# Two state decays moved behind the masks, one key decay moved ahead, and one quarter of a later group put in another order

## The chip, the cores and the metric

The kernel runs on one core of a Trainium2 chip. The metric is device time in microseconds (us) of one execution. The engines named below are TensorE (PE, matmuls; its weight loads are listed as PEld), VectorE (DVE), ScalarE (ACT), GpSimd (POOL) and SyncE (SP, here only a queue that issues DMAs). Each engine takes its instructions strictly in the order in which the code issues them, and waits at an instruction until what it reads is written and what it overwrites has been read.

## The reference

A linear attention with decay runs over 4 batches x 8 heads x 768 positions x 64 dimensions, and its output goes through a dense layer pair with a Mish between. Cut to what matters:

```
for b in range(nb):                                   # blocks of the sequence
    intra = (qb @ kb.T) * Dmask                       # masked scores inside the block
    intra = intra @ vb
    inter = (qb * lam_pow) @ kv_state                 # what the state of the blocks before gives
    out[block] = intra + inter
    kb_dec = kb * rev_pow                             # decayed keys
    kv_state = lam_block * kv_state + kb_dec.T @ vb   # decayed state
x = out as (3072 tokens, 512)
h = x @ w_in                                          # 512 -> 2048
out = (h * tanh(log1p(exp(h)))) @ w_out               # Mish, 2048 -> 512
```

## The kernel before

The sequence is cut into six **groups** `n` = 0 to 5 of 128 positions. In each group there are four **chunks** `b`, one for each batch, so that a group holds 512 tokens. The order of all work is written out by hand in one long body: what stands earlier in the code is issued earlier on each engine. There is no loop over equal stages that a scheduler reorders.

For a chunk `(n, b)` the attention goes in these steps. `decay_k` (L248) multiplies the keys by their decays into `kd`. `scores` (L255) puts eight small products into the PSUM banks `be` and `bo`, and two DVE multiplications with the mask `dm` (L260) write `sb`; these two are called the masks below. `outputs` (L276, L281) multiplies queries by the state and `sb` by the values into one bank, and a DVE multiplication (L284) writes `xn`; `xn` is turned on PE (L293, the function put aside in `later`) or by a DMA transpose (L287) into `xt`. `state` (L302) multiplies `kd` by the values; DVE adds the old state into `raw` (L310), and a last multiplication by `lbm` gives the new state `w0` to `w3` (L312), here called a state decay. In the second group (`n` = 1) the state decays of chunks 0 and 1 are put aside in the list `decays1` and run on DVE; those of chunks 2 and 3 run on POOL at once. `raw` has two buffers.

The first dense layer works on a group's 2048 features in units. In the second group each `two_units` puts eight matmuls of 256 columns into one of the banks `bA`, `bB`, `bC` and one Mish on ACT (L358) empties it. From the fourth group on the layer is done in four **quarters** (`set_of`, `set_step`) with seven products each in place of eight (Strassen's scheme): the steps `m1` to `m7` are four matmuls each (L412). `m5`, `m6`, `m7` and `m4` read differences of the input, `xsum0` to `xsum3` (L390, `x_sums`), of which the second and the fourth are built on earlier ones. Step `m5` copies its product to `p5` on ACT (L434), `m6` adds `p5` into bank C on DVE (L437), `m7` writes `c22` (L441).

The second dense layer of group `n` (`dense2`) runs beside the first layer of group `n` + 1 and the attention of group `n` + 2. It is a list of fourteen **halves**, eight matmuls each (L523), taken one after the other by `h(...)`: two each for the products 1, 2, 6, 5, 7, 3, 4. Products 6, 5, 7 and 3 read sums of the Mish outputs, `gsum0` to `gsum3` (L486, `sums`). The loop over `n` has one turn for each group; in the turn with `n` = 2 the fourth group's first layer starts, and it is the first turn whose quarters are of the kind "s" (seven products), after a turn whose last quarter was of the kind "p" (plain units). In that turn POOL prepares the keys of the fifth group (L248).

Of the kernel before, what the change touches and what calls it, by code (L numbers as in the profile page):

```python
# [7 lines left out]
F32 = mybir.dt.float32  # L8
# [5 lines left out]
def bc(ap, axis, n):  # L14
    shape = list(ap.shape)
    shape.insert(axis, n)
    return ap.unsqueeze(axis).broadcast_to(shape)
# [3 lines left out]
def kernel(  # L21
# [10 lines left out]
    nc = tc.nc  # L32
# [3 lines left out]
    JP = H // 2  # L36
# [14 lines left out]
    work = ctx.enter_context(tc.tile_pool(name="work", bufs=1))  # L51
    ps = ctx.enter_context(tc.tile_pool(name="ps", bufs=1, space=bass.MemoryType.PSUM))

    def bank(tag, shape, dtype=F32):
        return ps.tile([128] + shape, dtype, name=f"b{tag}", tag=f"b{tag}")
# [160 lines left out]
    def flat(t, j):  # L216
        return t[:, 2 * j : 2 * j + 2, :].rearrange("p h c -> p (h c)")
# [3 lines left out]
    def turn_pe(n, b, banks, which="kq", by_vector=False):  # L221

        srcs = (kn[n, b], qn[n, b])
        for src, name, to, tag in zip(srcs, ("kT", "qT"), (kT, qT), banks):
            if name[0] not in which:
                continue
            pt = bank(tag, [JP, C], F16)
            for j in range(JP):
                nc.tensor.matmul(pt[:, j, :], flat(src, j), ident, is_transpose=True,
                                 start=(j == 0), stop=(j == JP - 1))  # L230
            if b % 2 == 0:
                turned[name, n] = work.tile([128, 2 * JP, C], F16, name=name, tag=name, bufs=2)
            to[n, b] = turned[name, n][:, b % 2 * JP : b % 2 * JP + JP, :]
            if by_vector:
                nc.vector.tensor_copy(to[n, b], pt)
            else:
                nc.scalar.activation(to[n, b], pt, AF.Copy)
# [8 lines left out]
    def decay_k(n, b, eng):  # L246
        kd[n, b] = work.tile([128, H, D], F16, name="kd", tag="kd", bufs=4)
        eng.tensor_tensor(out=kd[n, b], in0=kn[n, b], in1=bc(lk, 2, D), op=ALU.mult)  # L248
# [23 lines left out]
    def outputs(n, b, turn=None, tag="z"):  # L272

        po = bank(tag, [H, D])
        for j in range(JP):
            nc.tensor.matmul(  # L276
                po[:, 2 * j : 2 * j + 2, :].rearrange("p h e -> p (h e)"), qT[n, b][:, j, :],
                wst[n, b][:, j, :], start=(j == 0), stop=False, skip_group_check=True)
        for j in range(JP):
            for t in range(2):  # L280
                nc.tensor.matmul(po[:, 2 * j + t, :], sb[n, b, t][:, j, :], vn[n, b][:, 2 * j + t, 0:D],  # L281
                                 start=False, stop=True, skip_group_check=True)
        xn = work.tile([128, H, D], F16, name="xn", tag="xn", bufs=2)
        nc.vector.tensor_tensor(out=xn, in0=po, in1=bc(lq, 2, D), op=ALU.mult)  # L284
        dst = x_tile(n)[:, :, b * C : (b + 1) * C]
        if turn is None:
            nc.sync.dma_start_transpose(out=dst, in_=xn.rearrange("p h c -> p (h c)"))  # L287
            return None

        def later():  # L290
            pt = bank(turn, [JP, C], F16)
            for j in range(JP):
                nc.tensor.matmul(pt[:, j, :], flat(xn, j), ident, is_transpose=True,  # L293
                                 start=(j == 0), stop=(j == JP - 1))
            nc.scalar.activation(dst, pt, AF.Copy)

        return later

    def state(n, b, tag, eng, later=False):
        pv = bank(tag, [JP, 128])  # L300
        for j in range(JP):
            nc.tensor.matmul(  # L302
                pv[:, j, :].rearrange("p (a e) -> p a e", a=2), flat(kd[n, b], j),
                vn[n, b][:, 2 * j : 2 * j + 2, 0:D], start=True, stop=True)
        w_new = const.tile([128, JP, 128], F16, name=f"w{b}") if n == 0 else wst[n, b]
        if n == 0:
            nc.vector.tensor_tensor(out=w_new, in0=pv, in1=lbm, op=ALU.mult)
        else:
            raw = work.tile([128, JP, 128], F32, name="raw", tag="raw", bufs=2)
            nc.vector.tensor_tensor(out=raw, in0=pv, in1=wst[n, b], op=ALU.add)  # L310
            wst[n + 1, b] = w_new
            decay = lambda: eng.tensor_tensor(out=w_new, in0=raw, in1=lbm, op=ALU.mult)  # L312
            return decay if later else decay()
        wst[n + 1, b] = w_new
# [3 lines left out]
    def h_tile(n):  # L318
        if n not in hsg:
            hsg[n] = work.tile([128, NKI, GT], F16, name="hsg", tag="hsg", bufs=2)  # L320
        return hsg[n]
# [22 lines left out]
    def next_bank():  # L344
        ring[0] += 1
        return "ABC"[ring[0] % 3]

    def two_units(n, ni, r):

        t = bank(next_bank(), [2, HC])  # L350
        cs = slice(r * HC, r * HC + HC)
        for u in range(2):
            for kc in range(NKC):
                m = (ni + u) % 4 * 128
                nc.tensor.matmul(  # L355
                    t[:, u, :], win[ni // 4][:, kc, m : m + 128], xt[n][:, kc, cs],
                    start=(u == 0 and kc == 0), stop=(kc == NKC - 1), skip_group_check=True)
        nc.scalar.activation(h_tile(n)[:, ni : ni + 2, cs], t, AF.Mish)  # L358
# [112 lines left out]
    def token_sum(n, i, part):  # L471

        if (n, i) not in gsum:
            gsum[n, i] = work.tile([128, HK, HC], F16, name=f"gsum{i}", tag=f"gsum{i}", bufs=1)
        w = HK // 2
        ks = slice(part * w, part * w + w)
        kh = slice(HK + part * w, HK + part * w + w)
        h = hsg[n]
        lo, hi = slice(0, HC), slice(HC, 2 * HC)
        a, b, op = (  # L480
            lambda: (h[:, ks, hi], h[:, kh, hi], ALU.add),
            lambda: (gsum[n, 0][:, ks, :], h[:, ks, lo], ALU.subtract),
            lambda: (h[:, ks, lo], h[:, ks, hi], ALU.subtract),
            lambda: (h[:, kh, lo], gsum[n, 1][:, ks, :], ALU.subtract),
        )[i]()
        nc.vector.tensor_tensor(out=gsum[n, i][:, ks, :], in0=a, in1=b, op=op)  # L486
# [187 lines left out]
    def sums(n, part, *which):  # L674
        for i in which:
            token_sum(n, i, part)

    ring[0] = 1
    later = {}

    def turn1(b, banks, eng=True):
        turn_pe(1, b, banks, "k")
        turn_pe(1, b, banks, "q", eng)

    def out1(b, turn, po, pv):
        later[b] = outputs(1, b, turn, po)
        return state(1, b, pv, nc.vector if b < 2 else nc.gpsimd, b < 2)

    first_units(8)
    for t in "kqv":  # L690
# [15 lines left out]
    decays1 = [out1(0, "G", "z", "H")]  # L706
# [7 lines left out]

    turn1(2, "ze")
    turn1(3, "oB")
    two_units(1, 0, 0)
    scores(1, 2)
    for decay in decays1:
        decay()  # L720
    decay_k(1, 2, nc.vector)
    two_units(1, 2, 0)
    two_units(1, 4, 0)
    scores(1, 3)
# [2 lines left out]
    two_units(1, 6, 0)  # L727
    later[2]()
    out1(3, "G", "e", "o")
    two_units(1, 8, 0)  # L730
    later[3]()
    two_units(1, 10, 0)
# [70 lines left out]
    def h(m=1):  # L803
        for _ in range(m):
            halves.pop(0)()
# [5 lines left out]
    KINDS = {1: "pppp", 2: "ssss", 3: "ssss", 4: "ssss"}  # L811
    WSUMS = {(1, 0): (1,), (1, 1): (3,)}

    for n in range(1, NG - 1):
# [32 lines left out]
        def fetch(*what):  # L847
            if m + 1 < NG:
                for t, bp in what:
                    load_pair(t, m + 1, bp)  # L850
# [6 lines left out]
        kinds = KINDS[n]  # L857
# [8 lines left out]
        def mm(i, *steps):  # L866
            for x in steps:
                set_step(sets[i], x)
# [5 lines left out]
        def opening(i):  # L874

            if kinds[i] == "s":
                mm(i, "m1")
                s_(i)
                mm(i, "seed")
                if i != 1:  # L880
                    settle()
            elif i == 0:
                s_(i)

        def closing(i):
            mm(i, "m7", "m3")
            owed.append(i)
# [35 lines left out]
            continue  # L923


        if "s" in kinds:
            x_sums(n + 1, 0, 1, 2, 3)
        opening(0)
        if m < NG:
            turn_dma(m, 1)  # L930
        if kinds[0] == "s":
            h(1)
            mm(0, "m2", "m5", "m6")
            sums(n, 1, 0, 1)
            h(1)
            o_(0)
            fetch(("k", 0), ("q", 0))
            closing(0)
        else:
            u(0)  # L940
            sums(n, 1, 0, 1)
            if n == 1:
                weight_sum(3, 0)
                weight_sum(3, 1)
            h(1)
            u(1)
            h(1)
            u(2)
            o_(0)
            fetch(("k", 0), ("q", 0))  # L950
            u(3)


        opening(1)
        h(1)
        if kinds[1] == "s":
            settle()
            mm(1, "m2")
# [121 lines left out]
```

## Time and profile before

| what | value |
|---|---|
| time, median of 3 runs | 205.52 us (205.46 to 206.92) |
| time of the profiled execution | 206.36 us |
| span from its first to its last instruction | 204.6 us |
| busy: PE, DVE, ACT, POOL | 193.8, 147.5, 98.5, 81.7 us |
| mean granted clock of TensorE | 0.999 |

A page of the profile lists busy times, shares by slices of the span, the chain of work that ended last, and groups of instructions. A row of the timeline gives the start and the length in us, the engine, the line, the operation with `out<-in`, and in brackets how long the engine had been idle before and on what. Buffer numbers are left out of names, so `w<-raw,lbm` stands for each of the four state decays, `p` for `p5` and `c` for `c22`. Lengths of matmuls include a tail in which the next one already runs; the distance of starts is what an instruction takes.

### The profile page before, as it was taken

The numbers are of one execution on the slowest core, as the hardware profiler recorded it, in microseconds if no ns is written. First come the engines' busy times: TensorE is split into PE (matmuls) and PEld (weight loads), VectorE is DVE, ScalarE is ACT, GpSimd is POOL, SyncE is SP. The second block draws the span as 40 slices with busy tenths as digits, with TensorE's granted clock in tenths as the row PEclk, the third lists the DMA queues.
The fourth block names the chain that finished last, engine by engine and source line by source line (L and its number), as shares of the span: only waits on it lengthen the run. The fifth ranks groups of instructions, "written<-read, shape, count | busy, mean of one in ns | idle before, by whom it ended". The sixth has DMA issues, their size and how long they took to land.

```text
span 204.6 us, 4668 instructions
## 1 busy us (share of the span) xinstructions
PE 193.8 (95%) x1931; PEld 149.1 (73%) x1931; DVE 147.5 (72%) x247; ACT 98.5 (48%) x176; POOL 81.7 (40%) x78
## 2 busy tenths in 40 slices
PE   7869998979999999999999999999999999999990
PEld 3657455768865556667668888988988988888890
DVE  6696557698896977589868698799588657179041
ACT  4775663728631125343245662465474484826300
POOL 7998452472272591648684368230000000000020
PEclk9999999999999999999999999999999999999999
DMA  8999999999999999699999999994113211003123
GB/s 129 137 142 204 175 177 156 162 207 194 142 141 131 223 167 176 159 108 115 161 212 194 137 77 130 172 211 112 29 26 80 77 54 53 0 3 113 47 100 104
DMA packets 109336, 26.26 MB, mean 128 GB/s; under 512 B 99458, under 2 KB 108802, under 8 KB 109314
## 3 DMA queue, kind: packets, MB, share of 16 engines
q0 software_dynamic: 77568, 13.37, 88.5%
q1 hardware_dynamic: 30704, 12.33, 29.0%
q10 hardware_dynamic: 1042, 0.26, 0.6%
q8 instruction: 15, 0.25, 0.5%
q14 instruction: 7, 0.06, 0.1%
HBM read 27.26 MB, written 6.29 MB: 164 GB/s over the span
## 4 chain that ended last, share of the span: by engine, by line
PE 76%; DMA 9%; POOL 7%; DVE 3%; ACT 2%; issue 1%; POOLq 0%; DVEq 0%; ACTq 0%
PE bG L523 15%; PE bH L523 13%; DMA vn<-in_v_dram 8%; PE bB L412 6%; PE bC L412 5%; PE bA L412 4%; PE bA L329 3%; PE bB L329 3%; PE be L255 2%; PE bC L355 2%; POOL win L96 2%; PE bC L329 2%; PE bz L281 2%; PE bA L574 2%; PE bA L355 2%; PE bB L355 2%
## 5 line engine op out<-in xcount | busy, mean ns | idle before, releaser
L312 POOL TENSOR_TENSOR w<-raw,lbm 128x512 f16<-128x512 f32 x14 | 20.4, 1458 | 43.0 <-DVE raw L310 42.8
L523 PEld LDWEIGHTS <-gsum 128*128 128x128 f16 x336 | 31.2, 98 | 4.3
L523 PEld LDWEIGHTS <-hsg 128*128 128x128 f16 x240 | 23.0, 98 | 4.4
L605 POOL TENSOR_TENSOR c<-p,u 128x512 f32<-128x512 f32 x1 | 1.3, 1272 | 58.7 <-DVE p L604 58.7
L260 DVE TENSOR_TENSOR sb<-be,dm 128x512 f16<-128x512 f32 x22 | 15.1, 686 | 8.8 <-PE bo L255 8.1
L523 PE MATMUL bH<-tsum,gsum 128*128 128x256 f16 x160 | 20.4, 273 | 0.0
L329 PEld LDWEIGHTS <-win 128*128 128x128 f16 x136 | 12.6, 98 | 10.3 <-DMA win<-in_moe_w_in_dram 0.5
L412 PEld LDWEIGHTS <-wsum 128*128 128x128 f16 x192 | 18.5, 98 | 2.1
L523 PE MATMUL bG<-wout,hsg 128*128 128x256 f16 x160 | 19.9, 273 | 0.0
L412 PEld LDWEIGHTS <-win 128*128 128x128 f16 x144 | 13.8, 98 | 2.2 <-issue 0.5
L486 DVE TENSOR_TENSOR gsum<-hsg 128x1024 f16<-128x1024 f16 x20 | 15.1, 759 | 0.0
L284 DVE TENSOR_TENSOR xn<-bz,lq 128x512 f16<-128x512 f32 x18 | 12.3, 686 | 3.7 <-PE bz L281 3.7
L260 DVE TENSOR_TENSOR sb<-bo,dm 128x512 f16<-128x512 f32 x22 | 15.0, 680 | 0.0
L355 PEld LDWEIGHTS <-win 128*128 128x128 f16 x128 | 12.0, 98 | 1.6
L87 POOL DMA_DIRECT2D kn<-in_k_dram x10 | 11.8, 1182 | 2.8 <-PE bB L329 1.5
L87 POOL DMA_DIRECT2D qn<-in_q_dram x10 | 11.7, 1170 | 1.7 <-PE bA L329 0.9
L87 POOL DMA_DIRECT2D vn<-in_v_dram x10 | 11.6, 1164 | 1.4 <-DMA win<-in_moe_w_in_dram 1.4
L412 PE MATMUL bA<-xt,win 128*128 128x256 f16 x80 | 12.0, 272 | 0.1
L416 ACT ACTIVATE hsg<-bC 128x512 f16<-128x512 f32 x10 | 5.9, 593 | 11.7 <-PE bC L412 11.7
L329 PE MATMUL bA<-xt,win 128*128 128x512 f16 x44 | 11.3, 380 | 0.0
L574 PEld LDWEIGHTS <-hsg 128*128 128x128 f16 x64 | 6.1, 98 | 6.8
L335 ACT ACTIVATE hsg<-bA 128x512 f16<-128x512 f32 x11 | 6.6, 597 | 9.2 <-PE bA L329 9.2
(189 smaller groups left out, 442.3 us busy)
## 6 DMA issues: line engine op xcount, KB each, us to landing
out_dram<-osum SPq DMA_DIRECT2D x23, 256.0 KB, 2.8
kn<-in_k_dram POOLq DMA_DIRECT2D x10, 256.0 KB, 9.0
qn<-in_q_dram POOLq DMA_DIRECT2D x10, 256.0 KB, 7.1
vn<-in_v_dram POOLq DMA_DIRECT2D x10, 256.0 KB, 8.6
wout<-in_moe_w_out_dram POOLq DMA_DIRECT2D x4, 512.0 KB, 15.4
win<-in_moe_w_in_dram POOLq DMA_DIRECT2D x3, 512.0 KB, 10.8
vz<-in_v_dram POOLq DMA_DIRECT2D x2, 256.0 KB, 6.8
kn<-in_k_dram POOLq DMA_DIRECT2D x3, 128.0 KB, 4.7
```

What stands on the lines that cost most here:

```text
L87: nc.gpsimd.dma_start(out=tile_, in_=rows(src, n, 2 * bp, 2))
L260: nc.vector.tensor_tensor(out=sb[n, b, t], in0=p_[t], in1=dm[:, t], op=ALU.mult)
L284: nc.vector.tensor_tensor(out=xn, in0=po, in1=bc(lq, 2, D), op=ALU.mult)
L312: decay = lambda: eng.tensor_tensor(out=w_new, in0=raw, in1=lbm, op=ALU.mult)
L329: nc.tensor.matmul(open_[n, ni][:, lo:hi], win[ni // 4][:, kc, (ni % 4) * 128 : (ni % 4) * 128 + 128], xt[n][:, kc, lo:hi], start=(opens a ...
L335: nc.scalar.activation(h_tile(n)[:, ni, :], open_.pop((n, ni)), AF.Mish)
L355: nc.tensor.matmul(t[:, u, :], win[ni // 4][:, kc, m : m + 128], xt[n][:, kc, cs], start=(u == 0 and kc == 0), stop=(kc == NKC - 1), skip_ ...
L412: nc.tensor.matmul(t[:, u, :], lhs, rhs, start=(fresh and u == 0 and kk == 0), stop=(kk == 1), skip_group_check=True)
L416: nc.scalar.activation(h_tile(o.n)[:, 4 * o.s + 2 * r : 4 * o.s + 2 * r + 2, t * HC : t * HC + HC], src, AF.Mish)
L486: nc.vector.tensor_tensor(out=gsum[n, i][:, ks, :], in0=a, in1=b, op=op)
L523: nc.tensor.matmul(t, lhs(kk, blk), rhs(kk)[:, lo:hi], start=(fresh and kk == 0), stop=(kk == HK - 1), skip_group_check=True)
L574: nc.tensor.matmul(po, hsg[n][:, ki, b * C : (b + 1) * C], wout[part][:, kk, :], start=(ki == 0), stop=(ki == NKI - 1))
```

## The change

Three edits. First, the two multiplications of `decays1` move from just behind the masks of chunk 2 to behind `out1(3, ...)`, that is behind the masks of chunk 3 and the outputs and states of both upper chunks; `decay_k(1, 2, ...)` moves ahead of the masks of chunk 2. Second, since `raw` of the lower chunks now lives until then, `raw` of chunks 2 and 3 gets buffers of its own, those of `p5` and `c22`, which are first used for their own purpose in the turn `n` = 2. Third, in that turn alone (`fresh`), the second parts of `gsum0` and `gsum1` and the masks come ahead of `x_sums`, and two of the halves come earlier: one moves from behind `m6` to between `m2` and `m5`, the next from behind `opening(1)` to ahead of `closing(0)`. No instruction is added or taken out on any engine.

```
-    def state(n, b, tag, eng, later=False):
+    def state(n, b, tag, eng, later=False, home=("raw", 2)):
...
-            raw = work.tile([128, JP, 128], F32, name="raw", tag="raw", bufs=2)
+            raw = work.tile([128, JP, 128], F32, name="raw", tag=home[0], bufs=home[1])
...
-        return state(1, b, pv, nc.vector if b < 2 else nc.gpsimd, b < 2)
+        return state(1, b, pv, nc.vector if b < 2 else nc.gpsimd, b < 2,
+                     ("raw", 2) if b < 2 else (("p5", "c22")[b - 2], 1))
...
     turn1(3, "oB")
+    decay_k(1, 2, nc.vector)
     two_units(1, 0, 0)
     scores(1, 2)
-    for decay in decays1:
-        decay()
-    decay_k(1, 2, nc.vector)
     two_units(1, 2, 0)
...
     out1(3, "G", "e", "o")
+    for decay in decays1:
+        decay()
     two_units(1, 8, 0)
...
+        fresh = kinds[0] == "s" and KINDS[n - 1][3] == "p"
+        if fresh:
+            sums(n, 1, 0, 1)
+            opening(0)
         if "s" in kinds:
             x_sums(n + 1, 0, 1, 2, 3)
-        opening(0)
+        if not fresh:
+            opening(0)
...
             h(1)
-            mm(0, "m2", "m5", "m6")
-            sums(n, 1, 0, 1)
-            h(1)
+            if fresh:
+                mm(0, "m2")
+                h(1)
+                mm(0, "m5", "m6")
+            else:
+                mm(0, "m2", "m5", "m6")
+                sums(n, 1, 0, 1)
+                h(1)
             o_(0)
             fetch(("k", 0), ("q", 0))
+            if fresh:
+                h(1)
             closing(0)
...
         opening(1)
-        h(1)
+        if not fresh:
+            h(1)
```

**DVE in the second group.** DVE's queue before, from the masks of chunk 2 (`sb_697`, `sb_699`) to the last `raw` of the group (chunk 3):

```order
L260 TENSOR_TENSOR sb_697<-be_687,dm_148 128x512
L260 TENSOR_TENSOR sb_699<-bo_688,dm_148 128x512
L312 TENSOR_TENSOR w0_410<-raw_602,lbm_134 128x512
L312 TENSOR_TENSOR w1_417<-raw_630,lbm_134 128x512
L248 TENSOR_TENSOR kd_703<-kn_119,lk_149 128x512
L260 TENSOR_TENSOR sb_735<-be_725,dm_148 128x512
L260 TENSOR_TENSOR sb_737<-bo_726,dm_148 128x512
L284 TENSOR_TENSOR xn_752<-bz_739,lq_150 128x512
L310 TENSOR_TENSOR raw_759<-bH_754,w2_436 128x512
L248 TENSOR_TENSOR kd_762<-kn_119,lk_149 128x512
L284 TENSOR_TENSOR xn_793<-be_780,lq_150 128x512
L310 TENSOR_TENSOR raw_800<-bo_795,w3_443 128x512
```

The same stretch of DVE's queue after the change, where `kd_676` is the decayed keys of chunk 2 and `sb_733`, `sb_735` are the masks of chunk 3:

```order
L248 TENSOR_TENSOR kd_676<-kn_119,lk_149 128x512
L260 TENSOR_TENSOR sb_699<-be_689,dm_148 128x512
L260 TENSOR_TENSOR sb_701<-bo_690,dm_148 128x512
L260 TENSOR_TENSOR sb_733<-be_723,dm_148 128x512
L260 TENSOR_TENSOR sb_735<-bo_724,dm_148 128x512
L284 TENSOR_TENSOR xn_750<-bz_737,lq_150 128x512
L310 TENSOR_TENSOR raw_757<-bH_752,w2_436 128x512
L248 TENSOR_TENSOR kd_760<-kn_119,lk_149 128x512
L284 TENSOR_TENSOR xn_791<-be_778,lq_150 128x512
L310 TENSOR_TENSOR raw_798<-bo_793,w3_443 128x512
L312 TENSOR_TENSOR w0_410<-raw_602,lbm_134 128x512
L312 TENSOR_TENSOR w1_417<-raw_630,lbm_134 128x512
```

The two decays have gone from the third and fourth place to the end, and the key decay from the fifth to the first. PE's order in the second group is the same in both.

**DVE in the fourth group's first quarter.** DVE's queue before, from the first difference of the input to `c22`; `sb_1717` and `sb_1719` are the masks of the fifth group's chunk 0:

```order
L390 TENSOR_TENSOR xsum0_1692<-xt_1336 128x512
L390 TENSOR_TENSOR xsum1_1694<-xt_1336,xsum0_1692 128x512
L390 TENSOR_TENSOR xsum2_1696<-xt_1336 128x512
L390 TENSOR_TENSOR xsum3_1698<-xt_1336,xsum1_1694 128x512
L260 TENSOR_TENSOR sb_1717<-be_1707,dm_148 128x512
L260 TENSOR_TENSOR sb_1719<-bo_1708,dm_148 128x512
L437 TENSOR_TENSOR bC_1741<-bB_1721,p5_1746 128x512
L486 TENSOR_TENSOR gsum0_1558<-hsg_1284 128x1024
L486 TENSOR_TENSOR gsum1_1560<-gsum0_1558,hsg_1284 128x1024
L284 TENSOR_TENSOR xn_1779<-bz_1766,lq_150 128x512
L441 TENSOR_TENSOR c22_1793<-bB_1721,p5_1746 128x512
```

The same stretch after the change:

```order
L486 TENSOR_TENSOR gsum0_1558<-hsg_1284 128x1024
L486 TENSOR_TENSOR gsum1_1560<-gsum0_1558,hsg_1284 128x1024
L260 TENSOR_TENSOR sb_1711<-be_1701,dm_148 128x512
L260 TENSOR_TENSOR sb_1713<-bo_1702,dm_148 128x512
L390 TENSOR_TENSOR xsum0_1717<-xt_1336 128x512
L390 TENSOR_TENSOR xsum1_1719<-xt_1336,xsum0_1717 128x512
L390 TENSOR_TENSOR xsum2_1721<-xt_1336 128x512
L390 TENSOR_TENSOR xsum3_1723<-xt_1336,xsum1_1719 128x512
L437 TENSOR_TENSOR bC_1754<-bB_1715,p5_1759 128x512
L284 TENSOR_TENSOR xn_1779<-bz_1766,lq_150 128x512
L441 TENSOR_TENSOR c22_1801<-bB_1715,p5_1759 128x512
```

The two sums and the two masks, four instructions, now stand ahead of the four differences. On PE the order of this quarter was m1, scores, half, m2, m5, m6, half, outputs, m7, m3, m1 of the next quarter, scores, state, half, m4; it is now m1, scores, half, m2, half, m5, m6, outputs, half, m7, m3, m1 of the next quarter, scores, state, m4. On ACT the copy of the first output of `dense2` (L545), which the earlier half releases, now stands ahead of the copy to `p5` (L434). POOL's and SP's orders are the same in both.

## The prediction

> **What bounds the kernel now.** I read the page's busy times and its chain first.
>
> ```profile
> PE 193.8 (95%) x1931; PEld 149.1 (73%) x1931; DVE 147.5 (72%) x247; ACT 98.5 (48%) x176; POOL 81.7 (40%) x78
> ...
> PE 76%; DMA 9%; POOL 7%; DVE 3%; ACT 2%; issue 1%; POOLq 0%; DVEq 0%; ACTq 0%
> ```
>
> PE carries three quarters of the chain, DVE only 3%. A change to DVE's order can pay only where PE waits for DVE, so the next view is PE's busy time by stretches (us, then PE's busy time and its instructions).
>
> ```profile
> 36.00:46.00 10.00, 8.69 (x115) 6.98 (x113) 8.41 (x15) 5.07 (x10) 6.01 (x6) 1.00 1.95 185
> 46.00:136.00 90.00, 90.00 (x874) 66.50 (x872) 73.05 (x114) 38.18 (x68) 48.38 (x39) 1.00 1.56 157
> 136.00:198.00 62.00, 61.89 (x621) 54.32 (x620) 39.94 (x67) 32.99 (x61) 1.90 (x2) 1.00 0.23 63
> ```
>
> In the stretch of the first edit PE is short of busy by 1.31 us; from 46 to 136 us, which holds the third edit's place (107 to 115), it is never idle, and from there to 198 us it is short by 0.11. So the first edit has something to win and the third, in this execution, nothing. The timeline of PE in the second group shows where the idle time lies.
>
> ```profile
> 40.19 0.23 PE L255 MATMUL be<-qT,kT 64*128 64x128 f16 x1
> ...
> 40.75 0.40 PE L281 MATMUL bz<-vn,sb 128*128 128x64 f16 x8
> 41.58 0.40 PE L302 MATMUL bH<-vn,kd 128*128 128x128 f16 x4 [0.44 <-DVE kd L248]
> 41.82 1.04 PE L355 MATMUL bC<-xt,win 128*128 128x256 f16 x8
> 43.38 0.40 PE L293 MATMUL bG<-ident,xn 128*128 128x128 f16 x4 [0.53 <-DVE xn L284]
> 43.61 0.39 PE L276 MATMUL be<-w,qT 128*128 128x128 f16 x4
> 43.84 0.40 PE L281 MATMUL be<-vn,sb 128*128 128x64 f16 x8
> 44.58 0.40 PE L302 MATMUL bo<-vn,kd 128*128 128x128 f16 x4 [0.34 <-DVE kd L248]
> ```
>
> Three waits, all for DVE: the keys of chunk 2, `xn` of chunk 2, the keys of chunk 3. By starts they are longer than the brackets say, since a matmul's length includes its tail. The chain of waits, which goes by distances, shows what each takes, and what DVE does meanwhile.
>
> ```profile
> 39.73 1.20 DVE w L312 x2
> ...
> 41.44 1.28 DVE sb L260 x2
> 42.73 0.60 DVE xn L284
> 43.32 0.60 DVE raw L310
> 43.92 0.61 DVE kd L248
> ...
> 44.58 0.40 PE bo L302 x4
> 44.97 0.87 PE bA L355 x8
> ```
>
> Eight matmuls of 256 columns take 0.87 us; four of 128, or the eight of L281, take 0.23 (43.38 to 43.61 to 43.84 above). So PE could have gone on at 40.75 + 0.23 = 40.98, at 41.82 + 0.87 = 42.69 and at 43.84 + 0.23 = 44.07, and lost 0.60, 0.69 and 0.51, **1.80 us** in all. DVE runs nearly without a break, 0.60 us for each instruction, and the first two in the chain's rows are the decays that the change moves.
>
> **The first edit.** The keys of chunk 2 go ahead of the masks, into an idle stretch of DVE:
>
> ```profile
> 37.11 0.43 DVE L235 COPY qT<-bB 128x512 f16<-128x512 f16 x1
> ...
> 38.01 0.23 PE L255 MATMUL be<-qT,kT 64*128 64x128 f16 x1
> ...
> 38.44 0.69 DVE L260 TENSOR_TENSOR sb<-be,dm 128x512 f16<-128x512 f32 x1 [0.90 <-PE bo L255]
> ```
>
> From 37.54 on DVE waits 0.90 us for scores that PE starts 0.43 before the mask (38.01). A key decay takes 0.68 with its tail, so it is done at 38.2 and the masks of chunk 2 don't move; its keys are in SBUF by then, since these scores read them turned. The masks end at 39.73 (where the chain's first row starts), and nothing now stands ahead of the masks of chunk 3. Their scores start at 40.19, so the first mask starts at 40.19 + 0.43 = 40.62, in place of 41.44. With 0.60 each: masks 40.62 and 41.22, `xn` 41.82 to 42.50, `raw` 42.42, keys of chunk 3 from 43.02 to 43.70.
>
> PE then: the keys of chunk 2 wait for nothing, so L302 comes at 40.98 in place of 41.58. The eight matmuls of L355 run from 41.20 to 42.07. The turning of `xn` (L293) starts 0.06 after `xn` ends, as before (43.32 to 43.38): at 42.56, a wait of 0.49 in place of 0.69. L293, L276 and L281 with 0.23 each take PE to 43.25, and L302 of chunk 3 starts at 43.70 + 0.06 = 43.76, a wait of 0.51, as before. That is **0.82 us earlier** than 44.58. So of the 1.80 us 1.0 stays: from the masks of chunk 3 on PE still waits for DVE at its rate of 0.60. The bounds: nothing won, if something else holds PE at 44.58, and 1.80, if all three waits went.
>
> What is late next: the two decays now run from about 44.8, beside POOL's decays of chunks 2 and 3. What such a meeting costs stands in these rows, POOL first:
>
> ```profile
> 45.80 1.65 POOL L312 TENSOR_TENSOR w<-raw,lbm 128x512 f16<-128x512 f32 x1
> ...
> 46.24 1.76 DVE L248 TENSOR_TENSOR kd<-kn,lk 128x512 f16<-128x512 f16 x1
> ...
> 48.37 0.42 DVE L375 TENSOR_TENSOR wsum<-wsum,win 128x512 f16<-128x512 f16 x1
> 49.50 0.69 DVE L260 TENSOR_TENSOR sb<-be,dm 128x512 f16<-128x512 f32 x1 [0.71 <-PE bo L255]
> ...
> 51.83 0.25 PE L281 MATMUL bz<-vn,sb 128*128 128x64 f16 x3
> ```
>
> This key decay starts while POOL multiplies and takes 1.76 in place of 0.68: it ends 0.55 after POOL. One of the moved decays will meet the second POOL decay in this way, in place of this `kd`: same price, 1.08, paid once in both. DVE has lost 0.4 us of the idle time that it used to take (0.90 before 38.44; now 0.3 there and 1.0 before 40.62), so it reaches the masks of the third group at about 49.0 (48.37 + 0.34 + 0.4, a little less), where their scores allow 49.50 - 0.82 = 48.68. They end at 50.2, and L281 wants them at 51.83 - 0.82 = 51.0. Cover 0.8 us: cost nothing. The new `raw` buffers cost nothing either: their next users come 60 us later. No DMA is moved, and POOL's and SP's order stays.
>
> The Trainium skill has a rule that speaks against this edit: in its page "SBUF — State Buffer", section "Who interferes with whom", a DVE instruction with two SBUF inputs blocks, or is blocked by, a GpSimd instruction that reads SBUF, for the whole of whichever came first. The rows above agree, 1.08 us of it. If both moved decays were blocked in full by it, DVE would be late by one more 1.08, the masks would end at 51.3, and PE would lose 0.3 of the 0.82; the sum below would then be 205.05.
>
> **The third edit.** PE and DVE in the fourth group's first quarter, with the two instructions on which the sums depend:
>
> ```profile
> 104.91 2.48 POOL L248 TENSOR_TENSOR kd<-kn,lk 128x512 f16<-128x512 f16 x2
> ...
> 106.48 0.60 ACT L335 ACTIVATE hsg<-bA 128x512 f16<-128x512 f32 x1 [1.14 <-PE bA L329]
> ...
> 107.91 0.42 DVE L390 TENSOR_TENSOR xsum<-xt 128x512 f16<-128x512 f16 x1 [2.42 <-DMA xt<-xn]
> 108.05 1.03 PE L523 MATMUL bG<-wout,hsg 128*128 128x256 f16 x8
> 108.37 0.42 DVE L390 TENSOR_TENSOR xsum<-xt,xsum 128x512 f16<-128x512 f16 x1
> ...
> 109.35 0.60 PE L412 MATMUL bC<-xsum,wsum 128*128 128x256 f16 x4
> ...
> 111.28 0.68 DVE L486 TENSOR_TENSOR gsum<-hsg 128x1024 f16<-128x1024 f16 x1
> ...
> 111.56 0.60 PE L412 MATMUL bB<-xsum,wsum 128*128 128x256 f16 x4
> ...
> 112.00 0.69 DVE L486 TENSOR_TENSOR gsum<-gsum,hsg 128x1024 f16<-128x1024 f16 x1
> ```
>
> On the clock of before: the sums need the last Mish, done at 107.08, and POOL's second key decay ends at 107.39. Blocked as above, `gsum0` ends at 107.39 + 0.55 = 107.94; `gsum1`, bound to it, ends 0.72 later (111.28 to 112.00), 108.66. Masks from 108.57 and 109.17, `xsum0` from 109.77 to 110.19, `xsum1` (0.46 behind it) to 110.65. PE used to want `xsum0` at 109.35 and had it 1.0 us early. Now a half (0.87) stands ahead of m5: it wants `xsum0` at 110.22 and `xsum1` at 110.66. With the 0.06 from DVE to PE that is a stall of 0.03 to 0.05. The cover of 1.0 us is gone, but no time with it: the same matmuls follow in another order, and m4 stands behind the same sum of work. On ACT the copy of the half's output now comes ahead of `p5`: it can start when the half is through (109.35 + 1.03 = 110.4) and takes 0.6 like the Mish of the row, `p5` follows until 111.6, and DVE's addition L437, of 0.7 like a mask, ends at 112.3; m7, which overwrites what it reads, is due at 111.56 + 0.87 = 112.43. No stall, by 0.1. I take **+0.05**; from below 0, since PE doesn't wait there now, from above see the second rival.
>
> **The sum.** The profiled execution took 206.36, 1.76 more than its span and 0.84 more than the median. 206.36 - 0.82 + 0.05 = 205.59; the same 0.77 off the median of 205.52 gives **204.75**, own range 204.4 to 205.1.
>
> **The rivals.** *The gain is taken back downstream (205.2 to 205.7).* PE may run ahead of transfers that keep their own time: the DMA share, the last but one column of the stretches, is over 1 until 136 us. The nearest one to fear is the queries and keys of the third group's upper half, turned by DMA:
>
> ```profile
> kT<-kn SPq DMA_TRANSPOSE x1, 4.3
> ...
> 54.53 1.32 SPq L242 DMA_TRANSPOSE kT<-kn  x1
> ...
> 62.19 0.23 PE L255 MATMUL be<-qT,kT 64*128 64x128 f16 x1
> ```
>
> The keys land at 58.8, 3.4 us ahead of their scores, so 0.82 does no harm; after 46 us PE hardly waited for anything. Chance 0.15.
>
> *The third edit costs more than the first wins.* The place is `gsum0` behind POOL's key decays: if they ran 0.75 us later than here, `gsum0` would be blocked in full, 1.08 in place of some 0.1, and m5 would stall 1.0 as its cover is gone. Then 205.52 - 0.82 + 1.0 = 205.7; it is slower than before once the stall exceeds 0.82, and with both sums blocked 206.7. For it: POOL's 2.48 us end right where the sums now begin. Against it: both engines shift together by the 0.82. Chance 0.13.
>
> *It wins more (203.7 to 204.3).* All three waits gone would give 205.52 - 1.80 = 203.7; and where `xt` lands over 1.0 us later than 107.9 in other executions, m5 stalls before and not after. The arithmetic of DVE's rate speaks against the first. Chance 0.12.
>
> **How the numbers follow.** The forecast has 0.60. The range of eight in ten goes from 203.9 to 206.0: it leaves out the far ends of the last two rivals. A measurement here tells 1% from nothing, 2.06 us: under 203.46 only if the whole 1.80 and more goes (0.03), over 207.58 only with three full stalls of the second rival (0.02), so 0.95 for within.
>
> **What would show it.** L302 of chunk 2 right behind L281 with no bracket; the masks of chunk 3 near 40.6; waits of about 0.5 before L293 and L302 of chunk 3; one of DVE's two L312 near 1.76; PE busy without a break from 46 us, m5 ahead of which `xsum0` ends within 0.1. It is wrong if PE waits at m5, m6 or L281 of the third group, or if a stretch later gains an idle time as long as the one that went.

## The result, and the profile after

| | before | after |
|---|---|---|
| median of 11 runs | 205.75 us | 204.83 us |
| ratio, 95% interval | | 0.9943, 0.992 to 0.9967 |
| time of the execution shown | 206.36 us | 204.73 us |
| its span | 204.6 us | 202.9 us |

By the ratio the change makes the kernel 0.57% faster, 1.17 us of 205.75 (0.7 to 1.6); the two medians are 0.92 us apart. 204.75 was forecast, 0.77 under the median known then. Ratios here and below leave out executions over 1.5% above the fastest of the same kernel, here one of 209.62 us.

PE's timeline after the change, in the second group from chunk 3's scores (L255) to the first scores of the third group:

```profile
39.42 0.23 PE L255 MATMUL be<-qT,kT 64*128 64x128 f16 x1
...
39.98 0.40 PE L281 MATMUL bz<-vn,sb 128*128 128x64 f16 x8
40.22 0.39 PE L302 MATMUL bH<-vn,kd 128*128 128x128 f16 x4
40.44 1.04 PE L355 MATMUL bC<-xt,win 128*128 128x256 f16 x8
41.80 0.40 PE L293 MATMUL bG<-ident,xn 128*128 128x128 f16 x4 [0.32 <-DVE xn L284]
42.03 0.39 PE L276 MATMUL be<-w,qT 128*128 128x128 f16 x4
42.25 0.40 PE L281 MATMUL be<-vn,sb 128*128 128x64 f16 x8
42.99 0.40 PE L302 MATMUL bo<-vn,kd 128*128 128x128 f16 x4 [0.34 <-DVE kd L248]
...
47.48 0.23 PE L255 MATMUL be<-qT,kT 64*128 64x128 f16 x1
```

The wait before the first L302 is gone: it starts 0.24 after L281. The two others are there, by starts 0.49 (41.80 less 40.44 + 0.87) and 0.51 (42.99 less 42.25 + 0.23). From chunk 3's scores to the second L302, that of chunk 3, it takes 3.57 us, 4.39 before (40.19 to 44.58): 0.82 less. DVE's timeline shows the rate that sets them, and the moved decays:

```profile
36.67 0.68 DVE L248 TENSOR_TENSOR kd<-kn,lk 128x512 f16<-128x512 f16 x1
37.67 0.69 DVE L260 TENSOR_TENSOR sb<-be,dm 128x512 f16<-128x512 f32 x1 [0.32 <-PE bo L255]
38.28 0.68 DVE L260 TENSOR_TENSOR sb<-bo,dm 128x512 f16<-128x512 f32 x1
39.85 0.69 DVE L260 TENSOR_TENSOR sb<-be,dm 128x512 f16<-128x512 f32 x1 [0.89 <-PE bo L255]
40.46 0.68 DVE L260 TENSOR_TENSOR sb<-bo,dm 128x512 f16<-128x512 f32 x1
41.06 0.68 DVE L284 TENSOR_TENSOR xn<-bz,lq 128x512 f16<-128x512 f32 x1
41.65 0.68 DVE L310 TENSOR_TENSOR raw<-bH,w 128x512 f32<-128x512 f32 x1
42.25 0.68 DVE L248 TENSOR_TENSOR kd<-kn,lk 128x512 f16<-128x512 f16 x1
...
44.05 2.36 DVE L312 TENSOR_TENSOR w<-raw,lbm 128x512 f16<-128x512 f32 x2
...
48.32 0.68 DVE L260 TENSOR_TENSOR sb<-be,dm 128x512 f16<-128x512 f32 x1
```

The key decay stands in the idle stretch, the masks of chunk 3 start 0.43 after their scores, and the two decays take 2.36 us together beside POOL's two (42.42 to 45.86), as the pair of key decays took in the same place before. The last row is the first mask of the third group.

Most of the rest of the difference between the two executions, 1.7 us of span less 0.82, stands ahead of what the edits reach: chunk 3's scores start at 40.19 before and at 39.42 after. PE's order up to there is the same, and two other kernels whose code is that of before up to there (`e2_third_only` and `e7_late_turn_before`, below) start them at 39.38 and 39.36. What differs in this head of the execution is, among others, how long PE waits for loads: at L281 it waits 0.9 us for values before and 0.3 after. This table gives, for the 14 executions of which there is a trace, the start of chunk 3's scores, the stretch from there to the third group's first scores, from there to m4 of the fourth group's first quarter, the part of this from m1 to m4, how long after m1 DVE begins with `xsum0`, and the stretch from m4 to PE's last matmul (all in us, by starts in PE's and DVE's timelines):

```
                       scores   to 3rd   to m4   m1 to   xsum0    m4 to
                       chunk 3  group            m4      after m1 the end
before                 40.19    8.88     65.37   7.28    0.76     85.11
after                  39.42    8.06     65.37   7.29    2.63     85.11
e1_first_only          39.01    8.06     65.37   7.29    0.70     85.11
e2_third_only          39.38    8.88     65.37   7.28    2.63     85.11
e3_keys_alone          39.69    8.28     65.36   7.28    0.86     85.11
e4_decays_alone        39.09    8.07     65.37   7.29    0.61     85.11
e5_no_waits            39.26    7.06     65.37   7.29    2.63     85.11
e6_keys3_early         39.88    7.55     65.55   7.29    2.63     85.11
e7_late_turn_before    39.36    8.88     65.78   7.70    1.27     85.11
e8_late_turn_after     39.39    8.07     65.37   7.29    2.63     85.11
e9_pool_longer         39.28    8.07     66.09   8.01    3.35     85.11
r_after                39.58    8.06     65.37   7.29    2.63     85.11
r_first_only           40.08    8.07     65.54   7.46    1.03     85.11
r_no_waits             39.00    7.06     68.87   7.29    2.63     85.11
```

The head varies by 1.2 us from execution to execution, the last 85 us not by 0.01. Between them each edit is read off to a few hundredths, more finely than any time tells it.

### The profile page after: what moved, and what is told of

It reads as the page before. It is cut to its first block, busy times and chain, and to the rows that moved or that the text cites. A ratio compares the mean times of both kernels' runs of the same rounds, so it can differ in the third digit from the quotient of the medians.

```text
span 202.9 us, 4669 instructions
## 1 busy us (share of the span) xinstructions
PE 194.7 (96%) x1931; PEld 150.1 (74%) x1931; DVE 148.0 (73%) x247; ACT 98.2 (48%) x176; POOL 81.8 (40%) x78
## 4 chain that ended last, share of the span: by engine, by line
PE 77%; DMA 9%; POOL 7%; ACT 2%; DVE 2%; issue 1%; POOLq 0%; DVEq 0%; ACTq 0%
PE bG L523 15%; PE bH L523 13%; DMA vn<-in_v_dram 8%; PE bB L412 6%; PE bC L412 5%; PE bA L412 4%; PE bA L329 3%; PE be L255 3%; PE bB L329 3%; PE bA L355 2%; PE bC L355 2%; PE bB L355 2%; POOL win L96 2%; PE bC L329 2%; PE bz L281 2%; PE bA L574 2%
## 5 line engine op out<-in xcount | busy, mean ns | idle before, releaser
L486 DVE TENSOR_TENSOR gsum<-hsg 128x1024 f16<-128x1024 f16 x20 | 15.6, 784 | 1.6 <-ACT hsg L335 1.6
L284 DVE TENSOR_TENSOR xn<-bz,lq 128x512 f16<-128x512 f32 x18 | 12.3, 685 | 2.9 <-PE bz L281 2.9
```

## The experiments

**The parts of the change apart.** *The first two edits without the third:* the fourth group's first quarter goes back.

```
-        fresh = kinds[0] == "s" and KINDS[n - 1][3] == "p"
-        ... (all that hangs on fresh)
+        x_sums(n + 1, 0, 1, 2, 3)
+        opening(0)
```

> The first two edits without the third (the fourth group's first quarter stands as before). Theory: the whole gain is the 0.82 us of the second group, so from the start of chunk 3's scores to its L302 it takes 3.57 us as in the changed kernel (4.39 before), from m1 of the first quarter to its m4 7.29 us as in both, and the time is 0.82 us or 0.4% under before (ratio 0.996). Rival: the third edit wins some 0.4 us of the measured 1.17 by itself; then this kernel stays 0.4 us above the changed one and a wait of PE at m5 or m6 shows up.

Measured: 3.57 to L302, 8.06 to the third group, m1 to m4 7.29; 205.29 us against 205.53, ratio 0.9964 (0.9935 to 0.9993). In the trace the first edit gives its 0.82 us alone. The time agrees, 0.74 us by the ratio, but with 0.1 to 1.3 it is too coarse to settle the rival: no wait at m5 or m6 is in the trace, and yet the ratio lies 0.2%, some 0.4 us, above that of the whole change.

*The third edit alone:*

```
     scores(1, 2)
+    for decay in decays1:
+        decay()
+    decay_k(1, 2, nc.vector)
```

(and these lines out of their new places, the `raw` buffers as before).

> The third edit alone (the second group stands as before). Theory: it moves no time, ratio 1.000 within 0.25%, m1 to m4 of the first quarter 7.29 us, the second group's stretch 4.39 us. Rival: it wins 0.4 us, ratio 0.998, since the input's last turned part lands late in some executions and m5 waits for it before. Second rival (the sums blocked by POOL's key decays): m1 to m4 longer by up to 1 us and ratio up to 1.005.

Measured: 4.39 to L302, 8.88 to the third group and 7.28, so nothing in the trace; 205.2 us, ratio 0.9979 (0.9958 to 1.0). The second rival is out. The first is not: the interval ends at no change, and its middle is where the rival put it.

*Of the first edit the keys alone:*

```
     turn1(3, "oB")
+    decay_k(1, 2, nc.vector)
     two_units(1, 0, 0)
     scores(1, 2)
     for decay in decays1:
         decay()
-    decay_k(1, 2, nc.vector)
```

> Of the first edit only the key decay of chunk 2 goes ahead of the masks; the two state decays stay behind the masks of chunk 2. Theory (DVE's rate of 0.60 us each sets the waits): the decays then run from the end of chunk 2's masks for 1.2 us and the masks of chunk 3 start 0.2 us after their scores allow, so the stretch from chunk 3's scores to its L302 takes 3.8 us (4.39 before, 3.57 with both). Rival: the decays were the whole cause, and this gives 4.39 still.

*Of the first edit the decays alone:*

```
     scores(1, 2)
-    for decay in decays1:
-        decay()
     decay_k(1, 2, nc.vector)
...
     out1(3, "G", "e", "o")
+    for decay in decays1:
+        decay()
```

> Of the first edit only the two state decays go to the end; the key decay of chunk 2 stays behind the masks of chunk 2. Theory: DVE then has an idle stretch of about 0.9 us ahead of chunk 3's masks which takes this key decay too, it ends 0.6 us ahead of its L302, and the stretch from chunk 3's scores to its L302 takes 3.57 us, as with both: moving the keys adds nothing to moving the decays. Rival: the keys' early place is what frees L302 of chunk 2, and a wait of up to 0.6 us before it stays.

One row of PE's timeline of each, the keys alone first: the L302 of chunk 3, to be set against the start of its scores in the table (39.69 and 39.09).

```profile
43.48 0.40 PE L302 MATMUL bo<-vn,kd 128*128 128x128 f16 x4 [0.34 <-DVE kd L248]
```

```profile
42.67 0.40 PE L302 MATMUL bo<-vn,kd 128*128 128x128 f16 x4 [0.34 <-DVE kd L248]
```

3.79 and 3.58 us, where 3.8 and 3.57 were expected. The keys alone are worth 0.60 of the 0.82; the decays alone are worth all of it. With the decays gone DVE has room for the key decay on either side of the masks of chunk 2. The key decay's new place adds nothing to the other.

**The waits that the change left.** *Chunk 3's key decay into DVE's next idle stretch too:*

```
     scores(1, 2)
+    decay_k(1, 3, nc.vector)
     two_units(1, 2, 0)
...
-    decay_k(1, 3, nc.vector)
```

> The changed kernel with chunk 3's key decay alone moved right behind chunk 2's masks. Theory: DVE takes it in the 0.89 us that it waits there for chunk 3's scores, so only the wait before L302 of chunk 3 goes: 0.51 us less from chunk 3's scores to the third group's first scores, the wait of 0.49 before L293 stays. Rival: something else (the values, a bank) holds L302, and nothing is won.

Measured: 7.55, 0.51 less than the changed kernel, as expected. 0.18 us of it is lost at 75.6 us in this execution, in a wait of PE that no other trace has; ratio to before 0.997 (0.9939 to 1.0), so that by the times this step isn't seen to win anything over the change.

*The turning of chunk 2's `xn` behind chunk 3's outputs as well:*

```
-    later[2]()
     out1(3, "G", "e", "o")
+    later[2]()
```

> The changed kernel, and in the second group also chunk 3's key decay right behind chunk 2's masks on DVE, and the turning of chunk 2's xn on PE behind the outputs and state of chunk 3 in place of ahead of them. Theory: the two waits that the change left, 0.49 and 0.51 us, are DVE's rate and both go, so the distance from chunk 3's scores to the third group's first scores falls by 1.0 us against the changed kernel (by 1.8 against before) and the time by as much: about 0.5% under the changed kernel, ratio to before 0.990 to 0.991. Rival (later stretches don't follow): the waits go but come back before the end, ratio 0.994 as the changed kernel.

PE's timeline from L281 of chunk 2 on:

```profile
39.82 0.40 PE L281 MATMUL bz<-vn,sb 128*128 128x64 f16 x8
40.05 0.39 PE L302 MATMUL bH<-vn,kd 128*128 128x128 f16 x4
40.28 1.04 PE L355 MATMUL bC<-xt,win 128*128 128x256 f16 x8
41.15 0.39 PE L276 MATMUL be<-w,qT 128*128 128x128 f16 x4
41.37 0.40 PE L281 MATMUL be<-vn,sb 128*128 128x64 f16 x8
41.61 0.39 PE L302 MATMUL bo<-vn,kd 128*128 128x128 f16 x4
41.83 0.39 PE L293 MATMUL bG<-ident,xn 128*128 128x128 f16 x4
42.05 1.04 PE L355 MATMUL bA<-xt,win 128*128 128x256 f16 x8
```

No bracket is left: 7.06 us, 1.82 less than before, the whole of the three waits. The time was 203.84 us against 205.41, ratio 0.9931 (0.99 to 0.9963), where 0.990 to 0.991 were expected, beside 0.9943 of the change: less than the 1.0 us that the trace has. It was run again beside the change:

> The version without the three waits again (chunk 3's keys early, the turning of chunk 2's xn behind the outputs of chunk 3, on top of the change). Theory: 1.0 us under the changed kernel and 1.6 to 2.2 under before, ratio 0.989 to 0.992. Rival: within 0.3 us of the changed kernel.

204.45 us, ratio 0.9934 (0.9906 to 0.9962), while the changed kernel on the same chip had

> The changed kernel again, beside the first two edits alone and the version without the three waits, on one chip. Theory: the second group gives 0.82 us and the third edit gives tenths in those executions alone in which the turned input lands over 0.2 us later than in the profile of before (it varied by 0.24 over four traces); so this kernel is 0.6 to 1.2 us under before and 0.0 to 0.4 under the first two edits alone. Rival: the third edit gives 0.4 us and more in most executions, and the distance of the two is 0.4 to 0.8.

204.51 us, ratio 0.9936 (0.9912 to 0.996). So the version without waits beats before, but the times don't tell it from the change: its rival, within 0.3 us, is what was measured. Its trace of the second time shows one way in which the gain goes, in the timeline of SP's queue and PE, and in the list of DMA issues (the last number is the time to landing):

```profile
55.60 1.54 SPq L242 DMA_TRANSPOSE qT<-qn  x1
...
62.08 0.21 PE L255 MATMUL be<-qT,kT 64*128 64x128 f16 x1 [2.83 <-DMA qT<-qn]
```

```profile
qT<-qn SPq DMA_TRANSPOSE x1, 6.4
```

The scores of the third group's chunk 2 waited 2.83 us for the turned queries, issued at 55.60 and landed 6.4 us later; in the kernel before the same transfer took 3.6. With another 0.6 us in a wait for DVE's keys behind it, 3.50 us were lost up to m4 (68.87 in the table). The traces show the margin shrink as PE gets ahead: the turned queries landed 2.5 us ahead of these scores before (56.06 + 3.6, scores at 62.19), 1.4 after the change (55.77 + 3.4, 60.61) and 0.4 in the first trace without the three waits (55.00 + 4.0, 59.43). The execution with the wait took 206.78 us. It is a single one: how much of the missing 1.0 us such landings explain in the other runs isn't shown.

**What the third edit is for.** *The kernel before, with the DMA that turns the last chunk of the fourth group's input issued behind the next store:*

```
-            nc.sync.dma_start_transpose(out=dst, in_=xn.rearrange("p h c -> p (h c)"))
+            go = lambda: nc.sync.dma_start_transpose(...)
+            go() if hold is None else hold.append(go)
...
             sums(n + 1, 0, 2, 3)
             h(1)
+            while turns:
+                turns.pop()()
             u(14)
```

> The kernel before, with one delay put in: the DMA that turns the last chunk of the fourth group's input is issued behind the next store on SP's queue, some 2.2 us later, so that it lands near 110.1 on the clock of before in place of 107.9. Theory: the third edit moved no time because PE had 1.0 us to spare there, and is a cover: without it m5 waits now for xsum0, some 1.2 us, and m1 to m4 of the first quarter takes about 8.5 us in place of 7.29. Rival: nothing is seen, since the landing isn't what the sums wait for.

*The same in the changed kernel:*

> The changed kernel with the same delay of the same DMA. Theory: the differences of the input stand 1.9 us later in DVE's order and m5 0.87 us later in PE's, so m5 waits only some 0.35 us, and m1 to m4 takes 7.6 to 7.7 us, 0.8 less than without the third edit. Rival (the order covers nothing): as long as in the kernel before with the delay, 8.5 us.

The two kernels took 7.70 and 7.29 us from m1 to m4, less than the 8.5 and the 7.6 to 7.7 expected: the delay came out smaller than meant. SP issued the transfer 2.14 us ahead of m1 in place of 4.51, but it landed in 3.4 us in place of 5.2, so `xsum0` begins 1.27 us after m1 in place of 0.76, 0.5 later and not 2.2. Whether m5 waits when it is 2.2 later was thus not tried. DVE and PE of the first (its lines stand one further down):

```profile
107.61 0.42 DVE L391 TENSOR_TENSOR xsum<-xt 128x512 f16<-128x512 f16 x1 [2.94 <-DMA xt<-xn]
...
108.53 0.60 PE L413 MATMUL bC<-xsum,wsum 128*128 128x256 f16 x4
...
110.28 0.69 DVE L438 TENSOR_TENSOR bC<-bB,p 128x512 f32<-128x512 f32 x1
...
110.50 0.40 PE L281 MATMUL bz<-vn,sb 128*128 128x64 f16 x8
111.02 0.60 PE L413 MATMUL bB<-xsum,wsum 128*128 128x256 f16 x4
...
112.20 0.68 DVE L284 TENSOR_TENSOR xn<-bz,lq 128x512 f16<-128x512 f32 x1
112.42 0.23 PE L255 MATMUL be<-qT,kT 64*128 64x128 f16 x1
...
112.94 0.38 PE L303 MATMUL bz<-vn,kd 128*128 128x128 f16 x4
```

m5 (108.53) does not wait. m7 does: 111.02 less 110.50 + 0.23 is 0.29. It may overwrite bank B only when DVE's addition (L437, here L438) has read it, and this stands on DVE behind all four differences and both masks: it starts 2.67 us after `xsum0` and ends at 110.97. A second wait is at the state of the fifth group's chunk 0 (L302, here L303). It writes the bank `bz`, which DVE's `xn` (L284) has to read first, and `xn` stands behind L437 and the two sums. L302 starts 0.06 after `xn` ends (112.88) and 0.52 after the scores. In the kernel before it stood right behind `xn` too:

```profile
112.61 0.69 DVE L284 TENSOR_TENSOR xn<-bz,lq 128x512 f16<-128x512 f32 x1
...
112.96 0.23 PE L255 MATMUL be<-qT,kT 64*128 64x128 f16 x1
...
113.34 0.38 PE L302 MATMUL bz<-vn,kd 128*128 128x128 f16 x4
```

That is 0.04 after `xn` ends (113.30) and 0.38 after the scores; with the third edit, which takes the two sums out from ahead of `xn`, it is 0.33 after them (112.29 to 112.62). So L302 had no margin before, and already waited 0.05. The cost of the delay was 0.42 us from m1 to m4, 0.28 at m7 and 0.14 at L302, and none with the third edit (7.29).

The threshold follows from L437. In the kernel before it starts 3.52 us after m1 (110.67), when `p5` is there, and the sums and `xn` follow it without a break. Once `xsum0` begins more than 3.52 - 2.67 = 0.85 us after m1, L437 starts later, and L302 with it, by as much as `xsum0` is late (1.27 costs 0.42; 1.03 costs 0.17, below; 0.86 costs nothing). m7 joins in only from about 1.0 us on (0.04 at 1.03, 0.28 at 1.27). By these numbers the edit is a cover: with it `xsum0` comes at 2.63 whatever the landing was here.

Whether that happens by itself was the question of the last run, the first two edits alone again:

> The first two edits alone again. Theory: 0.6 to 0.9 us under before (ratio 0.9955 to 0.997), and m1 to m4 of the first quarter 7.29 us. Rival: under 0.5 us.

It does: in this trace, without any delay put in, `xsum0` began 1.03 us after m1 and m1 to m4 took 7.46, where 7.29 was expected. The time was 205.17 us, ratio 0.9981 (0.996 to 1.0003), 0.42 us under the median of before where 0.6 to 0.9 were expected. Against the changed kernel's 0.9936 on the same chip that is 0.45% (the medians, 204.51 and 205.17, are 0.66 us apart), and 0.2% the first time (0.9964 against 0.9943): 0.4 to 0.9 us for the third edit by the times, 0 to 0.17 by the traces of before's order (0.76, 0.70, 0.86, 0.61 and 1.03 after m1). The times side with the rival stated for the repeat of the changed kernel, 0.4 to 0.8; the size, and what it comes from beyond the 0.17, stays open, since a head that varies by 1.2 us can shift such a comparison by some tenths.

**The price of a blocked sum.** *The changed kernel with one more key decay on POOL ahead of the two:*

```
                 if b == 0 and not last:
+                    if n == 2:
+                        extra = work.tile([128, H, D], F16, name="extra", tag="extra", bufs=1)
+                        nc.gpsimd.tensor_tensor(out=extra, in0=kn[m, 0], in1=bc(lk, 2, D), op=ALU.mult)
                     decay_k(m, 0, nc.gpsimd)
```

> The changed kernel with one more key decay on POOL (written to a buffer that nothing reads) ahead of the fifth group's two, so that POOL's row there ends about 1.0 to 1.1 us later. The second rival of the prediction says that then gsum0 is blocked by POOL for about 1 us more, the differences of the input follow as late, and m5 waits for them: m1 to m4 of the first quarter about 8.3 us in place of 7.29. Against it: DVE gets its turn between two of POOL's instructions, gsum0 ends where it did or at most 0.5 us later, and m1 to m4 takes 7.3 to 7.8 us.

DVE, PE and POOL of this kernel:

```profile
104.62 2.49 POOL L248 TENSOR_TENSOR kd<-kn,lk 128x512 f16<-128x512 f16 x2
...
105.38 0.83 DVE L486 TENSOR_TENSOR gsum<-hsg 128x1024 f16<-128x1024 f16 x1 [1.62 <-ACT hsg L335]
106.25 1.42 DVE L486 TENSOR_TENSOR gsum<-gsum,hsg 128x1024 f16<-128x1024 f16 x1
...
109.24 0.60 PE L412 MATMUL bC<-xsum,wsum 128*128 128x256 f16 x4 [0.58 <-DVE xsum L390]
```

Both had a part: `gsum0` got its turn between two of POOL's instructions and was no later than in the changed kernel, but `gsum1` met the next one and took 1.42 in place of 0.69. All after it came 0.72 later, m5 waited, and m1 to m4 took 8.01, 0.72 more. The second rival's mechanism is there; what it needs, POOL ending later against m1 (here by 1.45 us, where 1.0 to 1.1 were meant), was not in any trace of the changed kernel.

## Why the prediction was right, and where it was not

*The first edit* went as worked out, step by step: no wait before the first L302, 0.49 and 0.51 before the two others (0.49 and 0.51 in the text), 0.82 us in all. Two of its parts were tried alone and came out within 0.01 of what DVE's row of 0.60 us each gave. What the prediction did not see is that the decays alone would do.

*The decays' new place:* one of the two was blocked by POOL, as said (1.76 us, the other 0.68), and the masks of the third group began at 48.32, without a wait before them; nothing came of it.

*The third edit:* +0.05 was taken, and m1 to m4 shows next to nothing (7.29 against 7.28). Here are its rows after the change:

```profile
105.53 0.83 DVE L486 TENSOR_TENSOR gsum<-hsg 128x1024 f16<-128x1024 f16 x1 [1.62 <-ACT hsg L335]
...
108.20 0.42 DVE L390 TENSOR_TENSOR xsum<-xt 128x512 f16<-128x512 f16 x1
...
108.67 0.60 PE L412 MATMUL bC<-xsum,wsum 128*128 128x256 f16 x4
109.12 0.60 PE L412 MATMUL bB<-xsum,wsum 128*128 128x256 f16 x4
109.99 0.70 DVE L437 TENSOR_TENSOR bC<-bB,p 128x512 f32<-128x512 f32 x1 [0.25 <-ACT p L434]
...
110.89 0.60 PE L412 MATMUL bB<-xsum,wsum 128*128 128x256 f16 x4
```

m5 starts 0.05 after `xsum0` ends (108.62), so "within 0.1" held, and the row up to it came as worked out: both sums and `xsum0` end within 0.01 of the times in the text, on a clock 1.58 earlier. The stall at m5 is there too, 0.03: the half ahead of it starts at 107.77 and takes 0.87, m5 starts at 108.67. It doesn't show in the total because the edit also removes the 0.05 that L302 of the fifth group's chunk 0 lost to `xn` before. The prediction put such a gain at nothing, since PE's busy time showed no break there; a wait of 0.05 is hidden in the tail of the matmul before it. That the two nearly cancel is chance.

One step was wrong: that PE "had it 1.0 us early" in the kernel before. That is m5's margin alone. The tightest user of DVE's row was L302, through L437, the two sums and `xn`, with 0.1 us (0.86 less 0.76); m7, through L437, had some 0.24. So that a stall comes only where `xt` lands "over 1.0 us later", and at m5, was mis-sized and misplaced: L302 is later from 0.1 on. The third rival, that the change wins more, named a cause that a trace shows (a late landing of `xt`, 0.17 us), but had the instruction and the threshold wrong; the measured 1.17 against 0.77 may hold some of it. The forecast counted 0.77, the traces have 0.82, and the ratio gave 1.17 with 0.7 to 1.6: that the median of 204.83 comes so near to 204.75 owes something to luck, and says little about the third edit.

*Downstream:* PE ran from 44.5 to 134.5 without a break, and m4 to the end took the same 85.11, so nothing was taken back in that trace. The place that the first rival named, the third group's turned queries and keys, is where a later version did wait, 2.8 us in one execution. The margin of 3.4 us was that of the keys, from one landing; the queries, issued behind them, landed at 59.7, 2.5 us ahead of the scores, and their landing took from 3.3 to 6.4 us in the traces.

## What to carry to other kernels

Where PE waits for DVE, write down DVE's row with its fixed distance and move out of it what nobody needs soon; the gain is that row's shift at the waiting instruction (0.82), not the sum of the waits (1.80) nor the time of what was moved (1.20). A margin must be read at every user of the late thing, those that overwrite as well as those that read, and of what stands behind it in the same queue: 1.0 us at m5 hid 0.1 at a matmul that waits for `xn`, nine instructions further down DVE's row. When executions differ by a us in their head, take distances between two fixed instructions of the traces.

## What the runs showed of the hardware that was not expected

The same transfer of turned queries landed after 3.6 us in one execution and 6.4 in another, and a head of 40 us in which PE waits for loads varied from 39.0 to 40.2, while PE's last 85.11 us agreed within 0.01 over 14 executions. Of two DVE instructions beside a row of POOL's, the first ran between two of them (0.83 us) and the second was held up by one (1.42 in place of 0.69, ending 0.56 after POOL's row: 106.25 + 1.42 against 104.62 + 2.49). The page "SBUF — State Buffer" of the Trainium skill, section "Who interferes with whom", has whoever issues first take the port for the whole instruction; these rows agree.
